# A slot's rows requested two pieces later, plain heads in three groups, logits evicted first, and the values' products in the rows' order

## The chip, the cores and the metric

The kernel runs on one core of a Trainium2 chip. The metric is the device time of one execution in microseconds (us). A core has TensorE (PE; its weight loads are shown apart as PEld), VectorE (DVE), ScalarE (ACT), GpSimd (POOL) and SyncE (SP), which issues most of the transfers.

## The reference

Two parts stand one behind the other. The first is windowed causal attention (8 batches, 8 heads, 576 positions, 64 wide, window 64); the second is a mixture of experts over the resulting 4608 rows of 512, each row going to one of 8 experts.

```python
scores = scale * np.matmul(q, k.transpose(0, 1, 3, 2))
mask = (rel >= 0) & (rel < window)                     # rel = row - column, window 64
attn = softmax(np.where(mask, scores, -1e9))           # with 1e-9 added to the sum
x = matmul(attn, v).transpose(0, 2, 1, 3).reshape(B * S, H * D)
logits = x @ w_gate + modality_bias[modality_id]
e_idx = np.argmax(logits, axis=1)
gate_w = softmax(logits)[np.arange(N), e_idx]
for e in range(E):
    mask = e_idx == e
    h = np.maximum(x[mask] @ w1[e], 0.0)
    out[mask] = gate_w[mask, None] * (h @ w2[e])
```

w1 is 512x1024 and w2 1024x512 for each expert. The expert's products are computed in three parts each (high times high, high times low, low times high), so that the result has nearly fp32 precision.

## The kernel before

**Attention.** The 4608 rows are 72 blocks of 64, nine to a batch; two blocks are a pair (36 pairs), two pairs a group (18 groups, `G`). The main loop (`for s in range(NPR + 4)`) is a pipeline over the pairs: step `s` computes the products with the values for pair `s - 2` (`values`, then `values_out`, which divides by the sums and writes the row tile `xa`), the logits of pair `s - 3` (`logits`), the scores of pair `s` (`scores`, and `minima` on VectorE), the transposes of the probabilities of pair `s - 1` (`probs_t`, two sets of four, each copied out by ScalarE as `pT`), and the exponentials on ScalarE (`exps`), in three portions. It also turns the heads of group `G = s // 2 + 1`: `PARTS` has k's two parts in an even step and q's two in an odd one. The first of the two goes over TensorE (`heads_t`, four transposes) and a copy out of PSUM (`heads_out`).

**Heads.** `load_qk` loads the k or q of one group. Below group 8 (`QUARTERS`), all eight heads come as plain rows, two transfers for each batch that the group touches. From group 8 on only the first four heads do (`nh = HP`); the other four come as quarters in eight transfers of 32-column pieces for each batch touched, laid out so that one VectorE transpose (`turn_heads`) turns the whole second part. Groups 11, 13 and 15 (of those from 8 on) hold a batch's end, touch two batches, and so have twenty transfers for k and as many for q.

**Rows.** The rows of `xa` are kept in an order of 32-column pieces; with it a VectorE transpose of 32x32 blocks (`x_turn`) later gives the transposed row tile of a slot. `values` writes the heads in their natural order, and `values_out` puts them into the rows' order with two products, one for each half of a head. The logits select an expert (`route1` to `route3`), and GpSimd scatters each pair's rows to the expert's place in `xs_scratch` by an indirect transfer.

**Slots.** A slot is 256 rows of one expert. `slot_pieces` is a generator of TensorE work: `first(sl, k, i)` is an eighth of the first product (12 matmuls of 256 columns), `second(sl, k, t)` an eighth of the second (6 of 512 columns). A slot has 16 pieces. From step 12 (`FIRST`) on, every step takes four of them at fixed places (`gap`). A slot's rows are read from `xs_scratch` by `fetch`, which calls `load_slot`: a register load of the row number and five transfers, all on SP, into `xt` (one buffer). Ahead of them `fetch` has the VectorE instructions of the plan issued that give the row number (`tick(need - issued[0], table=True)`). Then `x_turn` turns the tile on VectorE, and `x_part` splits it into a high and a low part (`xh`, `xl`). The first slots (`EARLY`) are taken while attention runs, and the rest (`LATE`) behind it; `last` tells the generator which.

**Order.** The order of the instructions on each engine is written out by hand (`manual_schedule`); each engine runs its own list in order, and so does SP with its transfers. `weights(s)` is one step in loading, splitting and storing a piece of the first two experts' weights: it has the piece before stored (`split_lo`, VectorE), the next one's high part made (`split_hi`, ScalarE, line 114) and another loaded (`load_piece`, SP, lines 103 and 107). The PSUM pool `ps_t` has two banks; `turn_bank` hands them out from step 12 on to the logits, the two sets of probabilities, the rows of `x_t`, the heads' transposes and the ranks.

Lines that come up below: 266 `x_turn`, 287 the gate's copy out of `xt`, 313 `hl`, 467 TensorE's transposes, 561 `turn_heads`, 577 and 583 the plain and the quarter loads, 598 `heads_out`, 633 scores, 668 `pT`, 685 the values' products, 691 and 696 `values_out`, 713 and 718 the logits and their eviction.

Of the kernel before, what the change touches and what calls it, by code (L numbers as in the profile page):

```python
# [8 lines left out]
F32 = mybir.dt.float32  # L9
# [4 lines left out]
ALU = mybir.AluOpType  # L14
# [5 lines left out]
P = 128  # L20
W64 = 64
# [5 lines left out]
def tile_window_attn_moe(  # L27
# [240 lines left out]
    def slot_pieces():  # L268
# [140 lines left out]
        while True:  # L409
            nxt = None  # L410
            for k in range(1, NK):
                for i in range(2):
                    if (k, i) == ((1, 0) if last else (2, 1)) or k == 2 and i == 1 and nxt is None:
                        assert todo
                        nxt = fetch()
                    first(sl, k, i)
                    if k == NK - 1 and i == (0 if last else 1):
                        later.append(lambda: x_turn(nxt))
                    yield
                for t in range(2):  # L420
                    second(sl, k - 1, t)
                    if k == NK - 1 and nxt and t == 1:
                        x_part(nxt, 1)
                    yield
                    if k == NK - 1 and nxt and t == 0:
                        x_part(nxt, 0)
                        run_later()
            second(sl, NK - 1, 0)
            yield
            if nxt["nb"] == 1:  # L430
                break
            first(nxt, 0, 0)
            yield
            first(nxt, 0, 1)
            yield
            second(sl, NK - 1, 1)
            yield
            sl = nxt
# [103 lines left out]
    def new_qk(G, nm):  # L542
# [4 lines left out]
        else:  # L547
            qk[G, nm] = work.tile([P, 2, H, D], F32, name="qk", bufs=2)

    def plain(t, nh):  # L550

        return t.rearrange("p t h d -> p (t h d)")[:, 0:2 * nh * D].rearrange("p (t h d) -> p t h d", t=2, d=D)
# [12 lines left out]
    def load_qk(G, nm, blocks=range(GBLK), dma=nc.sync):  # L565

        t = qk[G, nm]
        x = q if nm == "q" else k
        i = blocks[0]
        while i <= blocks[-1]:  # L570
            b, g = divmod(GBLK * G + i, BPB)
            n = min(BPB - g, blocks[-1] + 1 - i)
            nh = H if G < QUARTERS else HP
            src = x[b, 0:nh, g * W64:(g + n) * W64].rearrange("h (p t) d -> p t h d", t=2)
            p0 = i * W64 // 2
            for par in range(2):
                dma.dma_start(out=plain(t, nh)[p0:p0 + n * W64 // 2, par], in_=src[:, par])
            u = slice(i * W64 // R32, (i + n) * W64 // R32)
            for h in range(nh, H):
                for c in range(2):  # L580
                    rows = slice((h % 2 * 2 + c) * R32, (h % 2 * 2 + c + 1) * R32)
                    src = x[b, h, g * W64:(g + n) * W64, c * R32:(c + 1) * R32]
                    dma.dma_start(out=by_heads(t)[rows, (h - nh) // 2, u, :],
                                  in_=src.rearrange("(u p) d -> p u d", p=R32))
            i += n

    def heads_t(G, nm, i, tp):


        src = plain(qk[G, nm], H if G < QUARTERS else HP).rearrange("p t (h a) d -> p t h (a d)", a=2)  # L590
        for h in range(2):
            for t in range(2):
                n = 2 * h + t
                turn(tp[:, n * P:(n + 1) * P], src[:, t, 2 * i + h])
# [79 lines left out]
        nc.gpsimd.tensor_scalar(out=rs, in0=sm, scalar1=1e-9, scalar2=None, op0=ALU.add)  # L674


    def values(p):
        st.pop((p, "s"))
        av = st[p, "av"] = ps_a.tile([P, H, D], F32, name="av")
        for u in range(H):  # L680
            a, hp = divmod(u, HP)
            pT = st[p, "p", a]
            for c in range(2):
                i = hp * P + c * W64
                nc.tensor.matmul(  # L685
                    out=av[c * W64:(c + 1) * W64, 2 * hp + a], lhsT=pT[:, i:i + W64],
                    rhs=(vo if c else ve)[p][:, 2 * hp + a, :], start=True, stop=True)

    def values_out(p):
        rs = st.pop((p, "rs"))  # L690
        nc.vector.reciprocal(out=rs, in_=rs)
        xa = st[p, "xa"] = xas[p % XBUF]
        av = st.pop((p, "av")).rearrange("p (c g) (a d) -> p a c g d", g=2, a=2)
        to = xa[:, 0:DM].rearrange("p (g a c d) -> p a c g d", g=2, a=2, d=R32)
        for a in range(2):
            nc.vector.tensor_tensor(  # L696
                out=to[:, a], in0=av[:, a],
                in1=rs.rearrange("p (c g) -> p c g", g=2)[:, :, :, None].broadcast_to([P, NC1, 2, R32]), op=ALU.mult)

    def x_t(p, xp):  # L700
        xa = st[p, "xa"]
# [337 lines left out]
    for s in range(NPR + 4):  # L1039
# [10 lines left out]

        if 2 <= s < NPR + 2:
            values(s - 2)
            values_out(s - 2)
        if 3 <= s < NPR + 3:
            logits(s - 3, turn_bank(s) if s != FIRST else ps_m.tile([P, 512], F32, name="y0"))
            if (s - 3) % GB == GB - 1:
                route1((s - 3) // GB)
        if s < NPR:
            scores(s)
            if s == FIRST:  # L1060
# [50 lines left out]
        if n_gap > 2:  # L1111
            if FIRST <= s < FIRST + 4:
                weights(s)
            gap(it, True)
        if heads and G >= QUARTERS:
            turn_heads(G, *heads[1])
        elif heads:
            tp = turn_bank(s)
# [288 lines left out]
```

## Time and profile before

| | |
|---|---|
| median of 3 runs | 633.24 us (632.9 to 634.61) |
| profiled execution | 633.95 us |
| its span, first to last instruction | 632.2 us |
| mean granted TensorE clock | 0.985 |
| TensorE busy | 601.1 us (95%) |
| VectorE, ScalarE, GpSimd busy | 390.4, 294.3, 139.5 us |
| share of 16 DMA engines, SP's queue | 44.6% |
| steps 2 to 11 (attention alone) | 18.2 to 74.4 us |
| steps 12 to 36 (attention and slots) | 74.4 to 347.9 us |
| the rest (slots alone, with the last logits) | 347.9 to 632.2 us |

In a timeline row stand the start, the duration, the engine, the line, the operation, the tiles (out<-in), the shape and the count, and in brackets the engine's idle time before it and what ended it. In a row of waits stand who waited and for what, then the total, the number and the longest. In a row of stretches stand the stretch and its length, then each engine's busy time with its number of instructions, then the granted clock, the share of the DMA engines and GB/s. TensorE's matmuls overlap, so that the distance between two starts, not the duration, is what one costs in a row of many.

### The profile page before, as it was taken

The numbers are of one execution on the slowest core, as the hardware profiler recorded it, in microseconds if no ns is written. First come the engines' busy times: TensorE is split into PE (matmuls) and PEld (weight loads), VectorE is DVE, ScalarE is ACT, GpSimd is POOL, SyncE is SP. The second block draws the span as 40 slices with busy tenths as digits, with TensorE's granted clock in tenths as the row PEclk, the third lists the DMA queues.
The fourth block names the chain that finished last, engine by engine and source line by source line (L and its number), as shares of the span: only waits on it lengthen the run. The fifth ranks groups of instructions, "written<-read, shape, count | busy, mean of one in ns | idle before, by whom it ended". The sixth has DMA issues, their size and how long they took to land.

```text
span 632.2 us, 17434 instructions
## 1 busy us (share of the span) xinstructions
PE 601.1 (95%) x6285; PEld 536.4 (85%) x6285; DVE 390.4 (62%) x1532; ACT 294.3 (47%) x923; POOL 139.5 (22%) x315
## 2 busy tenths in 40 slices
PE   8999879699999989999999999999999999999996
PEld 5888678588889869888888999999899999989985
DVE  3899988587877767867765365223323634876721
ACT  3899786556565645555545111111113422564411
POOL 6332422132032312222321220011011101102202
PEclk7999999989999989999999999999999999999999
DMA  8999855765467457456532232732062554688300
GB/s 163 204 236 244 216 133 153 175 169 126 101 176 180 107 148 167 120 117 143 137 92 59 77 101 70 223 110 51 28 190 68 167 167 117 191 243 245 122 13 25
DMA packets 182793, 88.10 MB, mean 139 GB/s; under 512 B 146426, under 2 KB 165424, under 8 KB 182576
## 3 DMA queue, kind: packets, MB, share of 16 engines
q1 hardware_dynamic: 174080, 67.46, 44.6%
q0 software_dynamic: 5888, 18.93, 8.0%
q8 instruction: 50, 0.82, 0.5%
q10 hardware_dynamic: 2736, 0.58, 0.5%
q14 instruction: 39, 0.32, 0.2%
HBM read 67.49 MB, written 23.91 MB: 145 GB/s over the span
## 4 chain that ended last, share of the span: by engine, by line
PE 50%; DVE 0%; issue 0%; POOL 0%; ACT 0%; POOLq 0%
PE y L326 23%; PE em L304 13%; PE sp L304 10%; PE tp L467 1%; PE y L377 1%; PE av L685 1%; PE sp L352 0%; PE em L352 0%; PE tp L713 0%; PE sp L633 0%; DVE xa L696 0%; POOL out_dram L390 0%; ACT pT L668 0%; POOLq L1284 0%; DVE y L388 0%
## 5 line engine op out<-in xcount | busy, mean ns | idle before, releaser
L326 PE MATMUL y<-Whi,hh 128*128 128x512 f32 x288 | 116.2, 403 | 0.0
L659 ACT ACTIVATE ss<-ss,mn 128x128 f32<-128x128 f32 x288 | 112.5, 396 | 5.2 <-DMA y<-in_moe_modality_id_dram 2.7
L326 PE MATMUL y<-Wlo,hh 128*128 128x512 f32 x288 | 113.6, 395 | 0.0
L326 PE MATMUL y<-Whi,hl 128*128 128x512 f32 x288 | 113.0, 392 | 0.0
L337 POOL DMA_INDIRECT out_dram<-y,id x36 | 39.8, 1104 | 235.2 <-DVE y L334 154.9
L313 DVE SCALAR_TENSOR_TENSOR hl<-em,hh 128x512 fp32r<-128x512 f32 x50 | 34.5, 689 | 87.2 <-ACT hh L312 86.6
L304 PE MATMUL em<-xh,Whi 128*128 128x256 f32 x400 | 83.8, 291 | 0.0
L304 PE MATMUL em<-xl,Whi 128*128 128x256 f32 x400 | 79.2, 279 | 0.0
L304 PE MATMUL em<-xh,Wlo 128*128 128x256 f32 x400 | 79.1, 279 | 0.0
L312 ACT ACTIVATE hh<-em 128x512 fp32r<-128x512 f32 x50 | 29.6, 591 | 105.3 <-PE em L304 101.4
L668 ACT COPY pT<-tp 128x512 f32<-128x512 f32 x57 | 32.3, 588 | 73.6 <-PE tp L467 73.5
L647 DVE CUSTOM_DVE_ANT_0 ss<-sp,masks 128x128 f32<-128x128 f32 x288 | 63.4, 285 | 5.0 <-PE sp L633 4.9
L326 PEld LDWEIGHTS y<-Whi,hl 128*128 128x128 f32 x288 | 54.7, 190 | 12.2
L304 PEld LDWEIGHTS em<-xh,Whi 128*128 128x128 f32 x400 | 62.5, 189 | 1.8
L326 PEld LDWEIGHTS y<-Whi,hh 128*128 128x128 f32 x288 | 54.6, 190 | 9.0
L326 PEld LDWEIGHTS y<-Wlo,hh 128*128 128x128 f32 x288 | 54.8, 190 | 8.5
L304 PEld LDWEIGHTS em<-xl,Whi 128*128 128x128 f32 x400 | 60.9, 188 | 0.1
L304 PEld LDWEIGHTS em<-xh,Wlo 128*128 128x128 f32 x400 | 60.8, 188 | 0.0
L659 ACT ACTIVATION_READ_ACCUMULATOR ss<-ss,mn 128x1 f32 x288 | 55.5, 193 | 0.0
L789 POOL DMA_INDIRECT xs_scratch<-xa,idx x36 | 36.3, 1009 | 74.7 <-DVE lm L732 21.6
L312 ACT ACTIVATE hh<-sp 128x512 fp32r<-128x512 f32 x22 | 13.2, 598 | 75.8 <-PE sp L304 75.8
L467 PE MATMUL tp<-ident_r,ss 128*128 128x128 f32 x236 | 36.1, 284 | 12.3 <-ACT pT L668 8.4
(242 smaller groups left out, 1199.8 us busy)
## 6 DMA issues: line engine op xcount, KB each, us to landing
xt<-xs_scratch SPq DMA_DIRECT2D x72, 128.0 KB, 3.0
vo<-in_v_dram SPq DMA_DIRECT2D x32, 256.0 KB, 3.0
y<-in_moe_w_dram SPq DMA_DIRECT2D x32, 256.0 KB, 3.4
vo<-in_moe_w_dram SPq DMA_DIRECT2D x24, 256.0 KB, 4.1
ss<-in_moe_w_dram SPq DMA_DIRECT2D x24, 256.0 KB, 4.4
xs_scratch<-xs_scratch SPq DMA_DIRECT2D x8, 514.0 KB, 5.9
pT<-in_moe_w_dram SPq DMA_DIRECT2D x16, 256.0 KB, 4.4
qk<-in_k_dram SPq DMA_DIRECT2D x18, 128.0 KB, 4.7
```

What stands on the lines that cost most here:

```text
L304: nc.tensor.matmul(out=hb[:, i * TP:(i + 1) * TP], lhsT=w[buf][:, c0:c0 + P], rhs=x[:, c * TP:(c + 1) * TP], start=(n == 0), stop=(n == le ...
L312: nc.scalar.activation(out=hh, in_=hb, func=AF.Relu),
L313: nc.vector.scalar_tensor_tensor(out=hl, in0=hb, scalar=0.0, in1=hh.bitcast(F32), op0=ALU.max, op1=ALU.subtract)))
L326: nc.tensor.matmul(out=sl["y", t], lhsT=h[:, i * TP + t * P:i * TP + (t + 1) * P], rhs=w[buf][:, c0:c0 + DM], start=(k == 0 and n == 0), s ...
L337: ins = nc.gpsimd.indirect_dma_start(out=out, out_offset=bass.IndirectOffsetOnAxis(ap=sl["id"][:, t:t + 1], axis=0), in_=y, in_offset=None ...
L377: nc.tensor.matmul(out=yp[:, cols], lhsT=sl["h", n][lo][:, c * P:(c + 1) * P], rhs=w[buf][:, c0 + cols.start:c0 + cols.stop], start=(m == ...
L467: nc.tensor.transpose(out=out_, in_=in_, identity=ident[p0:p0 + n, p0:p0 + n])
L647: nc.vector.tensor_tensor_reduce(out=ss[a][:, hp, :], in0=sp[a][:, hp * P:(hp + 1) * P], in1=mask, scale=-1.0 / 8.0, scalar=3.0e38, op0=AL ...
L659: nc.scalar.activation(out=ss[a][:, hp, :], in_=ss[a][:, hp, :], func=AF.Exp, bias=mn[:, h:h + 1], scale=-1.0, accum_out=sm[:, h:h + 1])
L668: nc.scalar.copy(out=pT, in_=pp)
L685: nc.tensor.matmul(out=av[c * W64:(c + 1) * W64, 2 * hp + a], lhsT=pT[:, i:i + W64], rhs=(vo if c else ve)[p][:, 2 * hp + a, :], start=Tru ...
L789: ins = nc.gpsimd.indirect_dma_start(out=xs, out_offset=bass.IndirectOffsetOnAxis(ap=idx[:, j:j + 1], axis=0), in_=xg[j], in_offset=None)
```

## The change

It has four parts.

1. The request of the next slot's rows (`fetch`), while attention runs, stands ahead of `second(sl, 1, 1)` and no longer ahead of `first(sl, 2, 1)`: two pieces later. `x_turn` stays where it was. Behind attention nothing moves.
2. A new function `quartered(G)` tells whether a group's second part comes as quarters: from group 8 on, unless the group holds a batch's end. So groups 11, 13 and 15 load all heads plain, with four transfers each for k and q, and turn their second parts on TensorE, with a copy on ScalarE (k) or VectorE (q).
3. In the steps behind `FIRST`, `values_out` comes behind the logits, their eviction and `route1`; up to `FIRST` it stays ahead of them.
4. `values` writes each head's product in two runs of 32 columns to the places that the rows' order gives them in the bank. `values_out` then needs one product over 512 columns, with the reciprocals written out once for each run of 32 (`rw`, 16 values a row).

```diff
@@ slot_pieces
-                    if (k, i) == ((1, 0) if last else (2, 1)) or k == 2 and i == 1 and nxt is None:
-                        assert todo
+                    if k == 1 and i == 0 and last:
                         nxt = fetch()
+                        turn_at = 0
                     first(sl, k, i)
-                    if k == NK - 1 and i == (0 if last else 1):
+                    if k == NK - 1 and i == turn_at:
                         later.append(lambda: x_turn(nxt))
                     yield
                 for t in range(2):
+                    if k == 2 and t == 1 and nxt is None:
+                        nxt = fetch()
+                        turn_at = 1
                     second(sl, k - 1, t)
...
+    def quartered(G):
+        return G >= QUARTERS and GBLK * G // BPB == (GBLK * G + GBLK - 1) // BPB
@@ load_qk
-            nh = H if G < QUARTERS else HP
+            nh = HP if quartered(G) else H
@@ heads_t
-        src = plain(qk[G, nm], H if G < QUARTERS else HP).rearrange("p t (h a) d -> p t h (a d)", a=2)
+        src = plain(qk[G, nm], HP if quartered(G) else H).rearrange("p t (h a) d -> p t h (a d)", a=2)
...
+    def by_block(x):
+        return x.rearrange("p h d -> p (h d)").rearrange("p (g a c d) -> p g a c d", g=2, a=2, d=R32)
@@ values
-                    out=av[c * W64:(c + 1) * W64, 2 * hp + a], lhsT=pT[:, i:i + W64],
-                    rhs=(vo if c else ve)[p][:, 2 * hp + a, :], start=True, stop=True)
+                    out=by_block(av)[c * W64:(c + 1) * W64, a, :, hp, :], lhsT=pT[:, i:i + W64],
+                    rhs=(vo if c else ve)[p][:, 2 * hp + a, :].rearrange("p (a d) -> p a d", a=2),
+                    start=True, stop=True)
@@ values_out
-        nc.vector.reciprocal(out=rs, in_=rs)
+        rw = small.tile([P, 2, 2, HP], F32, name="rw")
+        nc.vector.reciprocal(
+            out=rw, in_=rs.rearrange("p (c g) -> p g c", g=2)[:, :, None, :].broadcast_to([P, 2, 2, HP]))
         xa = st[p, "xa"] = xas[p % XBUF]
-        av = st.pop((p, "av")).rearrange("p (c g) (a d) -> p a c g d", g=2, a=2)
-        to = xa[:, 0:DM].rearrange("p (g a c d) -> p a c g d", g=2, a=2, d=R32)
-        for a in range(2):
-            nc.vector.tensor_tensor(
-                out=to[:, a], in0=av[:, a],
-                in1=rs.rearrange("p (c g) -> p c g", g=2)[:, :, :, None].broadcast_to([P, NC1, 2, R32]), op=ALU.mult)
+        nc.vector.tensor_tensor(
+            out=xa[:, 0:DM].rearrange("p (x d) -> p x d", d=R32),
+            in0=st.pop((p, "av")).rearrange("p h d -> p (h d)").rearrange("p (x d) -> p x d", d=R32),
+            in1=rw.rearrange("p g a c -> p (g a c)")[:, :, None].broadcast_to([P, 2 * H, R32]), op=ALU.mult)
@@ the main loop
             values(s - 2)
-            values_out(s - 2)
+            if s <= FIRST:
+                values_out(s - 2)
         if 3 <= s < NPR + 3:
             logits(s - 3, turn_bank(s) if s != FIRST else ps_m.tile([P, 512], F32, name="y0"))
             if (s - 3) % GB == GB - 1:
                 route1((s - 3) // GB)
+        if FIRST < s < NPR + 2:
+            values_out(s - 2)
...
-        if heads and G >= QUARTERS:
+        if heads and quartered(G):
             turn_heads(G, *heads[1])
```

## The prediction

> **What bounds the kernel now.** I read the page's first part, then the stretches of single steps, then TensorE's waits, and then, wait by wait, the timelines of the engines that ended them.
>
> ```profile
> span 632.2 us, 17434 instructions
> PE 601.1 (95%) x6285; PEld 536.4 (85%) x6285; DVE 390.4 (62%) x1532; ACT 294.3 (47%) x923; POOL 139.5 (22%) x315
> ...
> 74.39:85.23 10.84, 8.32 (x125) 7.51 (x124) 10.55 (x47) 8.75 (x35) 3.92 (x8) 1.00 0.65 175
> ...
> 97.47:107.47 10.00, 10.00 (x133) 9.03 (x132) 7.86 (x43) 5.63 (x21) 2.85 (x4) 1.00 0.70 176
> 117.94:136.29 18.35, 12.60 (x133) 10.71 (x132) 11.55 (x46) 8.50 (x31) 4.88 (x9) 0.81 0.61 146
> ...
> 220.61:235.78 15.17, 12.20 (x138) 10.33 (x137) 8.57 (x38) 6.46 (x22) 2.86 (x5) 0.89 0.51 140
> 277.93:287.93 10.00, 10.00 (x133) 9.03 (x132) 5.75 (x29) 5.00 (x20) 3.45 (x7) 1.00 0.68 153
> ```
>
> The stretches run from one pair's first product with the values to the next pair's: steps 12, 14, 16, 25 and 30. A step of the shared stage (attention beside the first slots) takes 10.00 us where TensorE never idles (steps 14 and 30). Step 16 takes 18.35 and step 25 takes 15.17, at a granted clock of 0.81 and 0.89. So the stage is TensorE's own work plus a list of stalls, and the change can pay only out of that list, or by TensorE's work.
>
> ```profile
> PE tp L467 <- ACT pT L668: 10.4, 7, 5.0
> PE tp L467 <- DVE lg L718: 3.8, 7, 1.4
> PE tp L467 <- DMA qk<-in_q_dram: 2.3, 2, 2.0
> PE sp L633 <- DVE se L775: 0.8, 1, 0.8
> ```
>
> These four rows of TensorE's waits between 74 and 348 us (total, times, longest) hold 17.3 of its idle time; the clock that drops after the two long ones adds to them. Behind 348 us TensorE is almost without gaps, and no edit changes that part's order, except that its first row loads come from the moved request.
>
> **Logits first (C).** In every step behind 12 the eviction of `lg` now stands ahead of `values_out` on VectorE.
>
> ```profile
> 238.07 0.88 DVE L696 TENSOR_TENSOR xa<-av,rs 128x256 f32<-128x256 f32 x2
> 238.87 0.15 DVE L718 TENSOR_TENSOR lg<-tp,bias_sel 128x8 f32<-128x8 f32 x1
> ...
> 239.17 0.52 PE L467 MATMUL tp<-ident_r,ss 128*128 128x128 f32 x3 [0.20 <-DVE lg L718]
> ...
> 181.72 0.59 ACT L668 COPY pT<-tp 128x512 f32<-128x512 f32 x1 [2.68 <-PE tp L467]
> 182.36 0.66 PE L467 MATMUL tp<-ident_r,ss 128*128 128x128 f32 x4 [0.68 <-ACT pT L668]
> 182.66 0.15 DVE L718 TENSOR_TENSOR lg<-tp,bias_sel 128x8 f32<-128x8 f32 x1
> ```
>
> In step 26 `lg` ends at 239.02, and the second set of probability transposes starts at 239.17: it takes the bank that the logits held. With the eviction ahead of the reciprocal and the two products it ends some 1.1 us earlier (238.07 to 238.87, and about 0.3 for the reciprocal), more than nearly all of the seven waits; I take 3.5 of their 3.8. In step 21 the second set starts at 182.36, 0.05 after the copy of the first set has ended (181.72 + 0.59) and ahead of `lg`: there it shares the first set's bank. The row of 10.4 is five such waits of 0.68, one of 5.0 (step 16) and one of 2.0 (step 12). Whether the earlier eviction makes the second set take the logits' bank there the trace can't say: between 0 and 3.4; one of the five goes with B, of the other 2.7 I take half, 1.4. VectorE must now wait for the logits (0.5 us behind the values' products) in steps where it is early; its row products then end later, but their reader `x_t` comes one scores' set and a piece later on TensorE, and the minima wait for the scores anyway. If VectorE were late in all steps, `x_t` would be next to wait. C: 4.9, bounds 3 to 7.
>
> **Plain heads (B).** With `QUARTERS` = 8, the groups 11, 13 and 15 hold a batch end. Each part's load (k or q) is now 4 issues on SP and not 20.
>
> ```profile
> 222.98 4.89 SPq L583 DMA_DIRECT2D qk<-in_q_dram  x8
> 227.91 1.26 SPq L577 DMA_DIRECT2D qk<-in_q_dram  x2
> ...
> 230.39 0.30 PE L467 MATMUL tp<-ident_r,qk 128*128 128x128 f32 x1 [2.01 <-DMA qk<-in_q_dram]
> 230.98 0.87 PE L467 MATMUL tp<-ident_r,qk 128*128 128x128 f32 x3 [0.29 <-DMA qk<-in_q_dram]
> ...
> 236.05 0.71 DVE L561 STREAM_TRANSPOSE qT<-qk 128x512 f32<-128x512 f32 x1 [2.67 <-DMA qk<-in_q_dram]
> ```
>
> Eight quarter issues take 4.89 us, so 16 fewer save SP 9.8 us a part. In group 13 the plain issues of the second batch (227.91) stand behind the quarters of the first, and TensorE stalls 2.01 + 0.29 for them in step 25. Ahead of them they go out some 4.9 us earlier, more than the stall. The clock of 0.89 over 15.17 us is worth (1 - 0.89) x 15.17 = 1.7 at most; of it I take 1.2. Step 25's wait of 0.68 for a late VectorE goes too, since VectorE no longer waits for quarters there. Gain 2.3 + 1.2 + 0.7 = 4.2.
>
> What it adds: four transposes on TensorE for each second part, six sets in all.
>
> ```profile
> 242.90 0.60 PE L467 MATMUL tp<-ident_r,qk 128*128 128x128 f32 x4
> 243.25 0.47 PE L326 MATMUL y<-Whi,hh 128*128 128x512 f32 x1
> ```
>
> A set holds TensorE from 242.90 to 243.25, 0.35, and the matmul behind it takes 0.08 more (0.47 against the usual 0.39): 0.43 x 6 = 2.6, all of it on TensorE's path, since these steps have no other idle time. The copies (about 0.6 each, one on ScalarE and one on VectorE) replace a VectorE transpose of the same size; both engines have room in the step (VectorE 5.75 of 10.00 in the last stretch above). If it is gone, the next logits wait for the bank. B: 4.2 - 2.6 = 1.6, bounds -2.6 to 2.5.
>
> **The later request (A).** Five row loads per slot and the register load ahead of them move past one weight piece on SP, sometimes two, but not past the next step's loads of v, k and q; the forced ticks on VectorE move with them.
>
> ```profile
> 109.53 3.87 SPq L211 DMA_DIRECT2D xt<-xs_scratch  x5
> 113.67 0.36 SPq L107 DMA_DIRECT2D y<-in_moe_w_dram  x1
> 114.28 0.34 SPq L103 DMA_DIRECT2D y<-in_moe_w_dram  x1
> ...
> 117.00 3.95 SPq L583 DMA_DIRECT2D qk<-in_k_dram  x8
> 121.21 2.46 SPq L103 DMA_DIRECT2D y<-in_moe_w_dram  x3
> ...
> 124.92 0.62 ACT L114 CAST Whi<-y 128x512 fp32r<-128x512 f32 x1 [5.66 <-DMA y<-in_moe_w_dram]
> ...
> SPq L211 <- DMA xs_scratch<-xa,idx: 8.4, 3, 4.5
> ```
>
> SP stands 4.5 us for the rows' scatter before it issues the rows at 109.53; the weights wait behind. ScalarE then stands 5.66 us at 124.92 for the piece issued at 121.21, and that is TensorE's 5.0 in step 16. Now the pieces of 113.67 and 114.28 go out while SP would have stood. But the rows can't go before 109.5 (the scatter is no earlier), and the piece of 121.21 still follows the rows, v and ten issues of k. It moves up by what left the queue ahead of it: 109.53 + 3.87 = 113.40 to 114.75, about 1.3. So of the 5.0 only 1.2 goes; the 0.8 at the scores (VectorE behind a late piece) goes too. A: 2.0, bounds -3 to 6.
>
> What it puts at risk is the rows' arrival ahead of `x_turn`:
>
> ```profile
> 207.87 0.19 POOL L287 COPY gate<-xt 128x2 f32<-128x2 f32 x1 [7.87 <-DMA xt<-xs_scratch]
> ...
> 208.50 1.29 DVE L266 STREAM_TRANSPOSE xt<-xt 128x512 f32<-128x512 f32 x2
> ```
>
> GpSimd's copy shows the landing, 0.63 ahead of the transpose, the tightest that I found. Here SP lags the program by more than a step, so it issues the rows only one weight piece later (0.6); and B takes away the lag that groups 11 and 13 put on SP. I cost it at nothing.
>
> **The rows' order (D).** VectorE's two products of 128x256 become one of 128x512, the reciprocal writes 16 values, not 8.
>
> ```profile
> L696 DVE TENSOR_TENSOR xa<-av,rs 128x256 f32<-128x256 f32 x72 | 30.6, 425 | 10.1 <-PE av L685 4.9 <-DMA xs_scratch<-xa,idx 1.0 <-PE sp L633 0.4
> ...
> L313 DVE SCALAR_TENSOR_TENSOR hl<-em,hh 128x512 fp32r<-128x512 f32 x50 | 34.5, 689 | 87.2 <-ACT hh L312 86.6
> ...
> 246.17:247.67 1.50, 1.15 (x32) 1.01 (x32) 1.00 0.67 151
> ...
> 44.65:74.39 29.74, 27.98 (x156) 1.00 0.95 234
> ```
>
> Two by 425 are 0.85 (0.88 in the pair at 238.07); the nearest row of the new size out of PSUM takes 0.69. So 0.19 less a step. It counts where VectorE bounds: step 12 has it busy 10.55 of 10.84, and steps 7 to 11 (last row, VectorE alone) 27.98 of 29.74. Some seven steps there give 7 x 0.19 = 1.3; further on it is cover. Bounds 0 to 2.3 (twelve steps).
>
> On TensorE the values' products (third row, line 685 alone: 32 matmuls, 1.15 us, beside 1.01 of weight loads) now write two runs of 32 columns, 128 apart. No row of this trace has a matmul with a broken output. Between nothing and each counting as two: 0 to 36 x 1.15 = 41 us. I take nothing, since the weight loads already fill 1.01 of the 1.15 and the runs are 32 long.
> [...]
>
> **The sum.** C 4.9 + B 1.6 + A 2.0 + D 1.3 = 9.8. The profiled execution took 633.95 (span 632.2 and 1.75 around it): 633.95 - 9.8 = 624.2. It stands 0.7 above the median of the runs, 633.24, from which the same gain gives 623.4; I say 624.
>
> **Rivals.** *The stalls move on.* TensorE gains at the logits and waits again: VectorE is still late, the second set stays in the first set's bank, the extra copies of B hold a bank. For it: step 16's reason stays in the queue, and a step can't go under 10.00. Against it: 10.00 is reached in steps whose VectorE has 7.86 of work. It leaves D, half of C and A's 0.8, less B's 2.6: about 2 off, 631 to 632.
>
> *The broken output costs TensorE time* (slower than before). One mechanism, line 685: 576 pairs of matmuls; it decides from 9.8 / 576 = 17 ns a pair, where a pair now takes 1.15 / 16 = 72 ns. Doubled it costs 41: 633.2 - 9.8 + 41 = 664; at half of that 644. [...]
>
> *The rows come late.* If they land five us later than now (two pieces of a step of 10 with four) at all six slots of the stage, the margin of 0.6, perhaps of 3 at others, is gone, VectorE stands about 2 us a slot ahead of `hl` and the minima, and TensorE behind it: 6 x 2 = 12, so 633.2 - 9.8 + 12 = 635. Against it: SP's lag decides the issue, not the program.
>
> **Chances.** Forecast 0.70; stalls move on 0.16; broken output 0.07; late rows 0.07. The measurement tells about 0.3%, 1.9 us. Faster: 0.70 and half of the second, 0.78; same 0.10; slower 0.12. The range: below, the upper bounds of C, B and A with D (7 + 2.5 + 6 + 1.3 = 16.8) give 616.4, and not all come together: 617; above it takes in the moved stalls, 633, and leaves out the two slower ones.
>
> **What would show it.** C: `lg` ahead of `rw` in each step, and TensorE's row for `lg` near zero; the 0.68 waits gone or still there. B: no quarter issues in groups 11, 13, 15, step 25 under 11 us at clock 1.00, TensorE's transposes of `qk` up by 24. A: step 16 at 15 to 17 us, ScalarE's wait for `y` down by 1 to 2 in all; `x_turn` with no wait for a DMA. D: line 685 still 1.15 us a step, one product of 0.69. Wrong it would be if line 685 takes over 1.4 us, if `xt` shows DMA waits, or if step 16 loses its stall whole.

## The result, and the profile after

| | before | after |
|---|---|---|
| median of four runs each, one chip | 633.07 us (632.88 to 634.61) | 622.82 us (621.75 to 625.21) |
| ratio to before, 95% interval | | 0.9838 (0.9802 to 0.9874) |
| profiled execution, span | 633.95, 632.2 us | 621.75, 620.0 us |
| mean granted TensorE clock | 0.985 | 0.995 |
| steps 12 to 36 | 273.5 us | 262.7 us |

The forecast was 624.0. In the changed kernel the lines have moved a little: 470 TensorE's transposes, 640 scores, 675 `pT`, 696 the values' products, 704 and 707 the reciprocal and the product of `values_out`, 730 the eviction of the logits, 787 the sums that the scores wait for.

First the head of the page of the changed kernel, then the stretches of its steps 12, 14, 16, 21, 24 and 25 (stretch and length, busy time by engine, granted clock, share of the DMA engines, GB/s):

```profile
span 620.0 us, 17351 instructions
...
PE 596.6 (96%) x6309; PEld 534.8 (86%) x6309; DVE 385.8 (62%) x1493; ACT 293.6 (47%) x926; POOL 138.6 (22%) x315
```

```profile
73.03:83.56 10.53, 8.11 (x125) 7.44 (x125) 10.21 (x44) 8.43 (x34) 4.09 (x8) 1.00 0.72 192
...
94.94:104.94 10.00, 10.00 (x133) 9.04 (x132) 7.10 (x36) 5.99 (x21) 2.86 (x4) 1.00 0.81 200
115.08:131.26 16.18, 11.54 (x134) 10.07 (x133) 10.03 (x43) 7.06 (x25) 4.30 (x8) 0.89 0.60 145
172.34:183.92 11.58, 10.85 (x142) 9.58 (x141) 8.57 (x36) 6.91 (x24) 3.50 (x8) 1.00 0.71 188
204.09:215.44 11.35, 10.67 (x137) 9.41 (x136) 8.54 (x42) 7.13 (x25) 3.51 (x6) 1.00 0.73 193
215.44:226.08 10.64, 10.64 (x141) 9.60 (x140) 9.31 (x44) 6.32 (x23) 2.88 (x6) 1.00 0.51 126
```

TensorE has 24 more transposes and yet is busy 4.5 us less. Of that 2.0 lies in steps 12 to 36 (253.62 for 255.57), where a clock of 0.81 in step 16 and 0.89 in step 25 had stretched it before (12.60 and 12.20 us busy, now 11.54 and 10.64); 1.8 lies ahead of step 2 (13.40 for 15.22, at a clock of 1.00 for 0.81). The changed kernel's second profile has 15.85 at 0.74 there, so that part is not the change's. Step 25 has gone from 15.17 us at a clock of 0.89 to 10.64 at 1.00, all of it TensorE's own work; step 16 from 18.35 at 0.81 to 16.18 at 0.89; a free step is 10.00 as before. Steps 21 and 24 have become longer, by 0.5 and 0.4. What TensorE still waits for between 74 and 340 us (total, times, longest):

```profile
PE tp L470 <- ACT pT L675: 8.1, 4, 4.6
PE tp L470 <- DVE lg L730: 0.5, 1, 0.5
PE y L725 <- DVE se L787: 0.4, 1, 0.4
```

The row for the logits' eviction is down from 3.8 to 0.5, the two for `qk` and for the scores are gone. Timeline rows of the changed kernel, in order of time: VectorE in step 15, the queue and its readers in step 16, the second set of probabilities in steps 21 and 24, and the rows of step 23:

```profile
107.37 0.14 DVE L730 TENSOR_TENSOR lg<-tp,bias_sel 128x8 f32<-128x8 f32 x1
107.45 0.23 DVE L704 RECIPROCAL rw<-rs 128x16 f32<-128x16 f32 x1
107.71 0.69 DVE L707 TENSOR_TENSOR xa<-av,rw 128x512 f32<-128x512 f32 x1
...
113.13 3.95 SPq L590 DMA_DIRECT2D qk<-in_k_dram  x8
117.32 2.08 SPq L103 DMA_DIRECT2D y<-in_moe_w_dram  x3
...
120.71 0.62 ACT L114 CAST Whi<-y 128x512 fp32r<-128x512 f32 x1 [5.79 <-DMA y<-in_moe_w_dram]
...
122.91 1.11 PE L470 MATMUL tp<-ident_r,ss 128*128 128x128 f32 x4 [4.64 <-ACT pT L675]
...
174.47 0.16 DVE L730 TENSOR_TENSOR lg<-tp,bias_sel 128x8 f32<-128x8 f32 x1
...
175.62 0.59 ACT L675 COPY pT<-tp 128x512 f32<-128x512 f32 x1 [2.74 <-PE sp L640]
...
176.26 0.66 PE L470 MATMUL tp<-ident_r,ss 128*128 128x128 f32 x4 [0.73 <-ACT pT L675]
...
196.97 2.44 SPq L211 DMA_DIRECT2D xt<-xs_scratch  x5
...
201.83 0.19 POOL L287 COPY gate<-xt 128x2 f32<-128x2 f32 x1 [7.11 <-DMA xt<-xs_scratch]
...
202.88 1.29 DVE L266 STREAM_TRANSPOSE xt<-xt 128x512 f32<-128x512 f32 x2
...
207.96 0.66 PE L470 MATMUL tp<-ident_r,ss 128*128 128x128 f32 x4 [0.68 <-ACT pT L675]
```

`lg` stands ahead of the reciprocal, and one product of 0.69 has taken the place of two. In step 16 the weight piece (117.32) still follows the ten k issues of group 9, ScalarE still stands 5.79 us for it and TensorE 4.64. In step 21 `lg` is out at 174.63, and the second set waits all the same until the first set's copy is done (175.62 + 0.59 = 176.21): it takes the first set's bank, not the logits'. In step 23 GpSimd's copy shows the rows there 1.05 before `x_turn` (201.83 for 202.88), which has no wait. The first slot turned behind step 12, in step 15, has less to spare: 0.37, where the kernel before had 3.28.

Where the 12.2 us of span went, step by step: start -0.5; steps 2 to 11 -0.8; 12 -0.3; 13 -0.9; 15 -0.3; 16 -2.2; 17 -0.5; 20 -0.6; 21 +0.5; 24 +0.4; 25 -4.5; 26 -0.4; 28 and 29 -0.5; 32 and 33 -0.9; 36 -0.7. The part behind step 36 is the same to 0.1 us (284.4 and 284.3). In the 14 profiles of this case the time before step 2 varies from 16.4 to 19.5 us, so its 0.5 says nothing of the change, and steps 2 and 7 together from 10.0 to 11.7, so not much of the 0.8 can be read here either.

### The profile page after: what moved, and what is told of

Same layout as the page of the kernel before. It is cut to its first block, busy times and chain, and to the rows that moved or that the text cites. A ratio compares the mean times of both kernels' runs of the same rounds, so it can differ in the third digit from the quotient of the medians.

```text
span 620.0 us, 17351 instructions
## 1 busy us (share of the span) xinstructions
PE 596.6 (96%) x6309; PEld 534.8 (86%) x6309; DVE 385.8 (62%) x1493; ACT 293.6 (47%) x926; POOL 138.6 (22%) x315
## 4 chain that ended last, share of the span: by engine, by line
PE 82%; ACT 3%; issue 1%; DVE 1%; DMA 1%; POOL 0%; POOLq 0%; ACTq 0%; DVEq 0%
PE y L326 32%; PE em L304 22%; PE sp L304 10%; PE tp L470 8%; PE av L696 4%; PE sp L640 3%; PE tp L725 2%; PE y L377 1%; ACT ss L666 1%; DMA y<-in_moe_w_dram 1%; PE sp L352 0%; PE em L352 0%; ACT pT L675 0%; DVE xt L266 0%; ACT Whi L114 0%
## 5 line engine op out<-in xcount | busy, mean ns | idle before, releaser
L696 PEld LDWEIGHTS av<-ve,pT 128*64 128x64 f32 x576 | 36.3, 138 | 12.9 <-issue 7.4
```

The lines of the kernel that those rows point to most:

```text
L696: nc.tensor.matmul(out=by_block(av)[c * W64:(c + 1) * W64, a, :, hp, :], lhsT=pT[:, i:i + W64], rhs=(vo if c else ve)[p][:, 2 * hp + a, :] ...
```

## The experiments

The diffs are against the changed kernel, that of `e12_late_alone` against the kernel before. Ratios are to the kernel before, measured beside each experiment on the same chip; its median was 634.96 beside `e1` to `e4`, 636.29 beside `e5` to `e8`, and 634.47 beside `e9` to `e12`.

**The changed kernel once more** (`e5_again`), beside `e6` to `e8`.

> The changed kernel once more, unaltered, so that steps 12, 16 and 21 of a second profile and the time on this chip can be set beside the others. Both theories: 621 to 625 us; if step 16 differs from 16.2 by over 1 us, the 2 us that the earlier runs put on the later request can't be read off one profile.

624.18 us (621.45 to 627.06), ratio 0.9812 (0.9781 to 0.9842). From step 12 on all steps but a few repeat to 0.02 us; 16 (16.26 for 16.18), 21 (12.18 for 11.58), 12 and the time before it (start of step 12 at 74.36 for 73.03) do not. `e2_no_plain` and `e7_plain13` (below) differ from the changed kernel only from group 11's loads on, behind step 18; yet their step 12 takes 14.60 and 10.40, and their step 16 takes 17.27 and 17.23. So nothing below 4.2 us is read from step 12 in that list, and nothing below 1.1 from step 16, whose length also goes with its clock (16.18 at 0.89, and 18.13 at 0.81 in `e8_stride8`; last section).

**Logits first, undone** (`e3_no_first`).

```diff
             values(s - 2)
-            if s <= FIRST:
-                values_out(s - 2)
+            values_out(s - 2)
...
-        if FIRST < s < NPR + 2:
-            values_out(s - 2)
```

> The changed kernel with values_out ahead of the logits again in all steps; the other three parts stay. My theory: the waits of TensorE for lg and for the first set's copy come back in steps 13, 15, 17, 20, 26, 28, 29, 32, 33 and 36: 5 to 6 us more. Rival: the one product (0.2 less a step) and VectorE's freedom from quarters removed most of these waits; then 1 to 2 us more.

629.47 us (628.67 to 630.39), ratio 0.9914 (0.9893 to 0.9936), against 0.9838 and 0.9812 with the part in. TensorE's waits in this kernel, and the second set that waits for the first copy in step 20 (step 36 has the same wait):

```profile
PE tp L470 <- ACT pT L675: 9.0, 6, 4.4
PE tp L470 <- DVE lg L730: 2.6, 4, 1.3
```

```profile
169.89 0.66 PE L470 MATMUL tp<-ident_r,ss 128*128 128x128 f32 x4 [0.68 <-ACT pT L675]
```

Waits for the logits go from one to four, and waits for `pT` from four to six. The steps 13, 15, 16, 17, 19, 20, 23, 25, 28, 29, 32, 33 and 36 are longer, 6.7 in all, and 5.8 without step 16, which varies by as much. So the earlier eviction is one of the two parts that carry the gain (plain heads is the other) and is shown by its own removal. Some of it shows in no wait of the list: steps 17, 19, 23, 29, 32 and 33 are 0.3 longer each. In all six `lg` ends 3.1 to 3.2 us into the step (2.1 to 2.3 in the changed kernel), and the second set starts right behind it, at 3.3 for 3.0. TensorE's matmuls overlap (in the trace before, a set of four lasts 0.60, and the matmul behind it starts 0.35 after the set does), so the trace counts only 0.1 of this as idle.

**The rows' order, undone** (`e4_no_order`): `values` writes heads of 64 columns one behind the other, and `values_out` has two products of 256.

```diff
-                    out=by_block(av)[c * W64:(c + 1) * W64, a, :, hp, :], lhsT=pT[:, i:i + W64],
-                    rhs=(vo if c else ve)[p][:, 2 * hp + a, :].rearrange("p (a d) -> p a d", a=2),
+                    out=av[c * W64:(c + 1) * W64, 2 * hp + a], lhsT=pT[:, i:i + W64],
+                    rhs=(vo if c else ve)[p][:, 2 * hp + a, :],
...
```

> The changed kernel with the values' products in the heads' natural order and two products on VectorE; the other three parts stay. My theory: 1.1 to 1.5 us more, all of it by step 14 (steps 6 to 13, where VectorE bounds); the values' 32 matmuls take 1.15 us in both. Rival 1: later steps lose too, since VectorE comes 0.2 later to the logits: 3 us more. Rival 2: the broken output costs TensorE time; then the 32 matmuls take less here and the run is not slower.

626.33 us (624.4 to 627.06), ratio 0.9857 (0.9832 to 0.9882). Steps 2 to 11 take 56.36 us (18.06 to 74.42), against 55.37 and 54.89 with the part in (the changed kernel and `e5_again`); behind step 12 only 16 and 21 differ, which vary anyway. But the 1.0 to 1.5 can't be read off these sums: `e1_no_late`, with the part in, takes 56.44, and `e8_stride8`, with two products, 55.13. The steps that repeat say more: 6 and 8 to 11 together take 30.46 to 30.49 in all four kernels with two products (the one before, this one, `e8_stride8`, `e12_late_alone`) and 29.3 to 30.3, 29.87 in the mean, in the ten with one. So the part is worth 0.6 in the mean there, where attention runs alone; the ratios can't tell it from nothing.

**Columns eight apart** (`e8_stride8`): an output in runs of one column and not of 32, so that no two neighbouring columns of a product are neighbours in the bank. `values_out` has two products again.

```diff
-                    out=by_block(av)[c * W64:(c + 1) * W64, a, :, hp, :], lhsT=pT[:, i:i + W64],
+                    out=av.rearrange("p h d -> p (h d)").rearrange("p (e h) -> p e h", h=H)[
+                        c * W64:(c + 1) * W64, :, 2 * hp + a], lhsT=pT[:, i:i + W64],
...
```

> The changed kernel, but each of the values' products writes its 64 columns 8 apart (no two neighbours), and VectorE divides with two products, gathering from there. If runs of neighbours matter to TensorE's writes, the 32 matmuls of a step take well over 1.15 us, up to 2.3, and the run 20 to 40 us more; if not, 1.15 us as before, and some 2 to 4 us more for the second product on VectorE.

625.44 us (623.8 to 626.42), ratio 0.9825 (0.9794 to 0.9856). The line of the values' products (times in ns: least, median, most), first in this kernel, then in the changed one, then in the one before:

```profile
L696 PE MATMUL av<-ve,pT x576: 222/222/271, 19.1 to 339.9; 128*64 128x64 f32 x192
```

```profile
L696 PE MATMUL av<-ve,pT x576: 222/222/271, 17.7 to 336.7; 128*64 128x64 f32 x192
```

```profile
L685 PE MATMUL av<-ve,pT x576: 222/222/270, 18.2 to 348.8; 128*64 128x64 f32 x192
```

Contiguous, in two runs of 32, or in single columns eight apart: the same, and a step's 32 products take 1.15 us in each. A rival of the prediction falls here for this size. The 2 to 4 us expected for the second product did not come either: the changed kernel, measured beside it (`e5_again`), has 624.18.

**The later request, undone** (`e1_no_late`).

```diff
-                    if k == 1 and i == 0 and last:
+                    if (k, i) == ((1, 0) if last else (2, 1)) or k == 2 and i == 1 and nxt is None:
                         nxt = fetch()
-                        turn_at = 0
+                        turn_at = 0 if last else 1
...
-                    if k == 2 and t == 1 and nxt is None:
-                        nxt = fetch()
-                        turn_at = 1
```

> The changed kernel with the request of the slot's rows back at its old place; the other three parts stay. My theory: the later request is worth what step 16 gained: step 16 goes from 16.2 us back to about 18.3, the other steps stay, the profiled time is about 624 (changed kernel 621.75), 2 us more. Rival: step 16's gain came from VectorE being earlier (logits first, one product) and from SP's shorter queue; then step 16 stays within 0.5 of 16.2 and the time within 1 us of the changed kernel.

624.01 us (621.82 to 625.57), ratio 0.9828 (0.9802 to 0.9854): not to be told from the changed kernel. By the ratios the time came out as the rival said. The profiled run (624.24) and step 16 (18.61) came out as the theory said, but the changed kernel's second profile has 623.69 too, and step 21 is 0.9 shorter here (10.65).

**The later request alone** (`e12_late_alone`), in the kernel before: the diff above the other way round, and nothing else.

> The kernel before with the later request alone; quarters, order of the logits and the two products as before. Theory of the prediction: 2 us less than before, in step 16. Rival, from the run without plain heads: SP, late by the quarters of group 11, issues the rows after one more weight piece, VectorE waits 3 to 5 us at x_turn and TensorE in step 24 behind it: step 24 at 15 to 17 us (10.9 before), and 1 to 5 us more than before in all.

635.61 us (632.86 to 637.12), ratio 1.0014 (0.9995 to 1.0033): no gain. Its steps 16, 24, 25 and 26, and `x_turn` of the slot whose rows are used in step 24:

```profile
117.71:134.60 16.89, 12.01 (x133) 10.37 (x132) 10.47 (x44) 7.17 (x25) 4.76 (x9) 0.80 0.59 144
208.71:223.11 14.40, 12.06 (x133) 10.17 (x132) 10.64 (x45) 6.80 (x23) 4.68 (x10) 0.88 0.46 108
223.11:236.21 13.10, 10.79 (x138) 9.24 (x137) 7.97 (x37) 6.49 (x23) 1.92 (x5) 1.00 0.47 126
236.21:247.93 11.72, 10.42 (x134) 9.01 (x133) 7.56 (x38) 5.23 (x20) 4.02 (x7) 1.00 0.71 157
```

```profile
210.44 1.30 DVE L266 STREAM_TRANSPOSE xt<-xt 128x512 f32<-128x512 f32 x2 [2.86 <-DMA xt<-xs_scratch]
```

It takes 1.5 less in step 16 (which varies by that much) and 2.1 less in step 25, and 3.5 more in step 24 and 1.3 more in step 26. The rows come late, as one rival said: VectorE stands 2.86 us for them.

**Plain heads, undone** (`e2_no_plain`): groups 11, 13 and 15 have quarters again.

```diff
-        return G >= QUARTERS and GBLK * G // BPB == (GBLK * G + GBLK - 1) // BPB
+        return G >= QUARTERS
```

> The changed kernel with quarters again in groups 11, 13 and 15; the other three parts stay. My theory: step 25 goes from 10.6 back to about 15 us with TensorE's wait for q of some 2.3 and the clock's drop, the six sets of transposes (2.6 us in steps 20, 21, 24, 25, 28, 29) go: about 2.4 us more in all. Rival: the rows' later request already freed SP ahead of group 13; then step 25 stays under 12 us, and the run is 2 to 2.6 us less than the changed kernel.

630.92 us (628.05 to 636.85), ratio 0.9943 (0.9915 to 0.9971). The loss of 7 to 8 us by the ratios is more than the part was priced at, and it does not lie where I expected it: step 25 is 11.07 and not 15, but step 24 is 16.96; steps 24 to 29 together are 7.5 longer than in the changed kernel. (Step 12 is 14.60; it is one of those that vary, and lies ahead of these groups' loads.) Stretches of steps 24 and 25, VectorE's wait for the rows, and TensorE's waits behind it:

```profile
207.24:224.20 16.96, 12.88 (x133) 10.79 (x132) 10.57 (x44) 7.26 (x25) 4.63 (x10) 0.80 0.56 131
224.20:235.27 11.07, 10.39 (x137) 9.19 (x137) 8.03 (x36) 6.39 (x23) 1.97 (x5) 1.00 0.49 128
```

```profile
210.72 1.30 DVE L266 STREAM_TRANSPOSE xt<-xt 128x512 f32<-128x512 f32 x2 [4.61 <-DMA xt<-xs_scratch]
```

```profile
PE tp L470 <- ACT pT L675: 10.1, 4, 4.8
PE sp L640 <- DVE se L787: 3.9, 2, 3.4
```

The rows are the ones that lie ready 1.05 ahead in the changed kernel. Here VectorE stands 4.61 us for them, TensorE 3.4 at the scores behind VectorE, and the clock falls to 0.80.

**Plain heads in group 13 alone** (`e7_plain13`): is it group 13's second batch, as I had argued, or group 11's quarters, which stand ahead of those rows?

```diff
-        return G >= QUARTERS and GBLK * G // BPB == (GBLK * G + GBLK - 1) // BPB
+        return G >= QUARTERS and G != 13
```

> The changed kernel with plain heads in group 13 alone (quarters in 11 and 15). Theory 1, from the prediction: groups 11 and 15 had no stall, so four sets of transposes less: 1.7 us less than the changed kernel. Theory 2, from the run without plain heads: group 11's quarters make SP late, the rows requested later land behind x_turn's place in step 23, VectorE waits 3 to 5 us and TensorE behind it in step 24: 2 to 5 us more than the changed kernel.

626.55 us (626.03 to 627.72), ratio 0.9845 (0.982 to 0.987). Step 25 is 10.64, but it was 11.07 with no plain heads at all, where TensorE comes late out of step 24 and finds q landed; so this run does not show group 13's own share. Step 24 is 16.37. Two of group 11's four runs of quarters, then the queue ahead of the rows and `x_turn`; below them group 11's load of k in the changed kernel:

```profile
159.53 4.23 SPq L590 DMA_DIRECT2D qk<-in_k_dram  x8
...
173.52 5.31 SPq L590 DMA_DIRECT2D qk<-in_q_dram  x8
...
196.19 6.29 SPq L590 DMA_DIRECT2D qk<-in_q_dram  x8
...
204.06 2.99 SPq L211 DMA_DIRECT2D xt<-xs_scratch  x5
...
209.21 1.30 DVE L266 STREAM_TRANSPOSE xt<-xt 128x512 f32<-128x512 f32 x2 [4.60 <-DMA xt<-xs_scratch]
```

```profile
157.57 2.08 SPq L584 DMA_DIRECT2D qk<-in_k_dram  x4
```

The eight issues of 6.29 us at 196.19 are not group 11's: they are q of group 12, which has quarters in the changed kernel too (3.96 us at 185.60). Group 11's k holds the queue from 158.48 to 169.97 here, 11.5 us where four plain issues take 2.1, and its q another 12.3 for 3.8. So group 12's quarters start 10.6 later, and the rows go out at 204.06 and not at 196.97; the changed kernel's queue stands idle from 190.19 until then. Group 11's plain heads, and the slack that they leave on the queue, are what keeps the rows in time.

**The same with the old request** (`e9_plain13_early`): the diffs of `e7_plain13` and `e1_no_late` together.

> Plain heads in group 13 alone, and the request of the rows back at its old place; logits first and the rows' order stay. Theory 1 (the later request makes the rows late once group 11's quarters hold SP): VectorE's wait of 4.6 us at x_turn and TensorE's of 3.4 in step 24 go, step 24 is 11.4 us or less, the profile 5 us under that of plain heads in group 13 with the later request (627.52): 621 to 623. Theory 2 (group 11's quarters make it late by themselves): step 24 stays near 16 and the time at 626 to 627.

625.29 us (622.95 to 629.31), ratio 0.9861 (0.9826 to 0.9896). Step 24 takes 14.45, and `x_turn` waits:

```profile
209.63 1.30 DVE L266 STREAM_TRANSPOSE xt<-xt 128x512 f32<-128x512 f32 x2 [2.61 <-DMA xt<-xs_scratch]
```

That lies between the two theories. In the changed kernel group 11's quarters make the rows late with either request (2.61 us); the later request adds 2.0 (4.60).

**Plain heads in group 9 as well** (`e6_plain9`). Step 16's weight piece follows the quarters of group 9, which holds no batch's end; plain, it has two issues a part and not ten, and costs TensorE eight transposes more.

```diff
-        return G >= QUARTERS and GBLK * G // BPB == (GBLK * G + GBLK - 1) // BPB
+        return G >= QUARTERS and G != 9 and GBLK * G // BPB == (GBLK * G + GBLK - 1) // BPB
```

> The changed kernel with group 9 plain too (it loads in steps 15 and 16). My theory: what is left of step 16's stall (4.6 us and the clock behind it) is the weight piece behind group 9's eight quarter issues of k, 3.9 us of SP; with them gone the stall falls under 1 us, step 16 to 11 or 12 us, two sets of transposes cost 0.86: 3.5 to 4.5 us less than the changed kernel. Rival: the piece waits for its buffer or for the DMA engines, the stall stays; then 0.5 to 1 us more.

621.32 us (619.5 to 623.37), ratio 0.9769 (0.9746 to 0.9792). Its step 16, the queue and ScalarE there, and TensorE's wait:

```profile
115.72:128.46 12.74, 10.70 (x138) 9.43 (x137) 9.57 (x42) 7.68 (x26) 3.77 (x8) 1.00 0.62 164
```

```profile
112.50 1.92 SPq L584 DMA_DIRECT2D qk<-in_k_dram  x2
114.67 2.64 SPq L103 DMA_DIRECT2D y<-in_moe_w_dram  x3
...
118.76 0.62 ACT L114 CAST Whi<-y 128x512 fp32r<-128x512 f32 x1 [3.19 <-DMA y<-in_moe_w_dram]
...
120.95 0.66 PE L470 MATMUL tp<-ident_r,ss 128*128 128x128 f32 x4 [2.04 <-ACT pT L675]
```

The wait falls from 4.64 to 2.04, the clock stays at 1.00, and step 16 is 3.4 us shorter than in the changed kernel (step 17 is 0.55 longer by the added transposes). So the queue's order is shown to be most of what was left in step 16; I had expected a wait under 1 us and a step of 11 to 12. ScalarE still stands 3.19 for the piece.

**The remaining two combinations**: plain heads in 9 and 13 only with the old request (`e10_plain9_13_early`), and plain heads in 9, 11, 13 and 15 with the old request (`e11_plain9_early`).

> Plain heads in groups 9 and 13 alone, the request at its old place; logits first and the rows' order stay. If the later request only matters through the row loads' place on SP, this takes the 3.5 us of plain heads in group 9 in step 16 and saves four sets of transposes (1.7 us) that groups 11 and 15 don't need: 618 to 620 us, the fastest of all. If the old request costs its 2 us in step 16 here too: 620 to 622.

> Plain heads in groups 9, 11, 13 and 15, the request at its old place; logits first and the rows' order stay. Beside the same with the later request (621.32 median, step 16 at 12.7 us) it prices the later request alone where no group holds SP: theory of the prediction, 2 us more, in step 16; rival, within 1 us and step 16 within 0.7 of 12.7, so that the later request is worth nothing that can be told.

`e10_plain9_13_early`: 622.04 us (618.98 to 623.93), ratio 0.9807 (0.9777 to 0.9837); just past the upper of the two expectations. Step 24 is 12.86, with `x_turn` standing 2.45 us for its rows, so that the spared transposes of groups 11 and 15 are paid for there: that wait is again behind group 11's quarters. `e11_plain9_early`: 620.49 us (617.14 to 621.2), ratio 0.9773 (0.9744 to 0.9801), the same as `e6_plain9`. Against `e6_plain9`, with the later request, step 16 is 1.9 longer (14.65, at a clock of 0.88) and step 12 is 2.9 longer (13.27 for 10.40, where `x_turn` stands 1.2 us for its rows), but step 12 starts 2.1 earlier and step 21 is 0.9 shorter (10.65 for 11.58). So the time is as the rival said and step 16 as the theory said; but its wait is 2.12 us, that of `e6_plain9` 2.04, and the difference lies in the clock, 0.88 in the one step and 1.00 in the other (last section). These two, with four groups plain, are the fastest kernels measured, 0.4 to 0.7% under the changed one by the ratios; their intervals and that of `e5_again` still overlap.

## Why the prediction was right

The time, 622.82, is 1.2 under the forecast, and the profiled execution came down by 12.2 where the sum said 9.8, with 0.5 of it ahead of step 2. The mechanisms of the early eviction and of the shorter queue are borne out; that the sum came so near is in part luck, since one of its terms is worth nothing that can be measured, one half of what it said, and one far more.

**Logits first.** Forecast 4.9. Of the 3.8 for `lg`, 3.3 went. Of the five waits of 0.68, three went (steps 25, 29 and 36); without this part step 36 has its wait again and step 20 one too, while 25 and 29 stay without: so two fall to it, as I had taken (1.4), one of them in another step. Its removal costs more than these, 5.8 by the steps without step 16 and 4.8 to 6.5 by the ratios, since it also brings the 0.3 in six steps that the list of waits leaves out: the term was about right, or too small by up to 1.6. What I could not say the built programs answer, for each use of the two banks has its bank fixed there, before anything runs. The second set has the first set's bank in steps 16, 21, 24, 25, 29 and 36 of the kernel before, in 16, 21 and 24 of the changed one, and in 16, 20, 21, 24 and 36 with this part undone. TensorE's waits for `pT` behind step 12 lie in just these steps; the long one of step 16 is among them, because the first set's copy stands behind ScalarE's wait for the weight piece. So the second set can stay in the first set's bank although `lg` is out long before (1.6 us in step 21). That much of the rival in which the stalls move on came true. Why the build chooses the banks so stays open.

**Plain heads.** Forecast 4.2 - 2.6 = 1.6. Step 25 came down by 4.5 with one added set in it, more than worked out, and the price of 0.43 a set was right: steps 20, 28 and 29 take 10.34, 10.02 and 10.18 in `e7_plain13`, where they have no such set, and 10.78, 10.46 and 10.66 in `e5_again`, where they have one. With the other five sets at 0.43 that is 2.4 net. But the step of the argument that says where the gain lies was incomplete. I counted group 13's second batch; group 11 has no stall of its own in the trace before, and I gave it only a cost. `e2_no_plain` and `e7_plain13` show that its quarters hold the queue some 18 us longer (11.5 and 12.3 for 2.1 and 3.8), and that in the new kernel the rows of step 23 would be 4.6 us late behind them. By the ratios the part is worth 7 to 8 us inside the change, not 1.6 and far outside the bounds that I gave it, -2.6 to 2.5.

**The later request.** Forecast 2.0, as 1.2 of step 16's wait and 0.8 at the scores. Step 16 came down by 2.2 and the 0.8 is gone, but the wait fell only from 4.99 to 4.64, and ScalarE's own wait did not fall (5.66 and 5.79): the piece goes out 3.9 earlier (117.32 for 121.21) mostly because the whole step starts 2.9 earlier. So of the 2.2 the wait is 0.35, the scores 0.8, and the rest TensorE's own work, 11.54 for 12.60, at a clock of 0.89 for 0.81. In eight profiles with the later request and group 9 in quarters step 16 took 16.2 to 19.4, in three with the old one 18.4 to 19.3; step 21 took 11.6 to 12.8 with it, 10.65 to 11.8 without: in `e1_no_late` and `e11_plain9_early`, at 10.65, the built program gives the second set of step 21 the logits' bank, in the changed kernel the first set's. So the term of 2.0 was right in size for this profile only by chance: by the ratios (0.9838 and 0.9812 with, 0.9828 without; 0.9769 with, 0.9773 without) the part is worth nothing that can be measured, and alone it is worth nothing either (1.0014). Its risk was named rightly, "B takes away the lag that groups 11 and 13 put on SP": where B is not there (`e12_late_alone`, `e2_no_plain`) the rows are 2.9 and 4.6 late. The rival had priced that at 2 us in six slots; it is one slot of the stage that pays, with 3.5 to 5.6 us in one step.

**The rows' order.** Forecast 1.3; 0.6 in the mean in the five steps of attention alone that repeat, so the term was about twice too big. I had named the reciprocal's 16 values for 8 and left them out of the sum. The reciprocal's groups, before and after:

```profile
L691 DVE RECIPROCAL rs<-rs 128x8 f32<-128x8 f32 x36 | 7.0, 194 | 0.4
```

```profile
L704 DVE RECIPROCAL rw<-rs 128x16 f32<-128x16 f32 x36 | 8.8, 244 | 0.4
```

So by the means 0.11 a step is saved (0.85 + 0.194 - 0.691 - 0.244) and not 0.19, which over five to seven steps is 0.5 to 0.8. The values' products cost nothing more, as I had taken it: 222 ns in the median of line 696 in the changed kernel, and 222 with the columns eight apart (`e8_stride8`), as in the kernel before. My 41 us for each product counting as two, and the 664 and 644 of the rival, were an estimate from the 1.15 us of a step; no run shows any of it.

## What to carry to other kernels

Where one queue issues everything in order, as SP's does here, a transfer's place behind many small issues can decide when it lands (the rows of step 23 went out at 204.06 us in `e7_plain13` and at 196.97 in the changed kernel), and shortening the queue can matter most for a transfer that waits for nothing yet (these rows are there 1.05 us ahead in the changed kernel; in `e2_no_plain` VectorE stands 4.61 us for them): ask for every part of a change what it protects, not only which wait it removes. A step's wait was worth more than its own length where the clock fell behind it (step 25 came down by 4.5 us without its waits of 2.01, 0.29 and 0.68, at a clock of 1.00 for 0.89), and behind like waits it fell in one profile and not in another (0.88 with 2.12 us in `e11_plain9_early`, 1.00 with 2.04 in `e6_plain9`), so one profile does not price such a wait. Where a pool has two banks, read from the built program which use gets which. Undo each part of a bundle by itself, and do it alone as well: here one part was priced at 2 us by the rows of before and is worth 7 inside the change, and another nothing that can be measured in either place.

## What was not expected of the hardware

TensorE wrote its 64 columns in single elements eight apart as fast as in one run (222 ns, 1.15 us for 32 products beside 1.01 of weight loads); larger outputs were not tried. The clock did not follow the length of a wait alone: it stayed at 1.00 in a step with a wait of 2.04 us (`e6_plain9`), was 0.89 with one of 4.64, and 0.80 with one of 4.42 in `e3_no_first`; before the change it was 0.89 with 2.01 and 0.29 one behind the other.

The clock's own records, and stretches cut at their bounds, show more. Two stretches of step 16 in the changed kernel, then two in `e6_plain9`:

```profile
118.92:122.33 3.41, 0.00 (x0) 0.00 (x0) 0.45 (x1) 1.62 (x4) 0.00 (x0) 1.00 0.89 235
122.33:125.74 3.41, 2.83 (x9) 2.45 (x10) 3.38 (x21) 1.88 (x7) 0.00 (x0) 0.50 0.75 155
```

```profile
117.11:120.52 3.41, 1.81 (x44) 1.38 (x40) 2.07 (x9) 1.76 (x4) 0.00 (x1) 1.00 0.87 249
120.52:123.93 3.41, 2.98 (x20) 2.67 (x21) 3.36 (x22) 2.25 (x7) 0.00 (x0) 1.00 0.79 181
```

In all 14 profiles the granted clock is 1.00 or 0.50 and, between 65 and 350 us, changes only on a grid of 3.41 us that lies elsewhere in each profile. Step 16's 0.89 in the changed kernel is one interval at half (1 - 0.5 x 3.41 / 16.18), 0.80 in `e3_no_first` two (1 - 0.5 x 6.83 / 17.13). Counted over the 14 profiles, an interval at full clock in which TensorE was busy for 45% or less was followed by one at half in all 17 cases; at 52% or more in none; in between, in three of seven. In the kernel before and the changed one the intervals followed by one at half were busy for 20%, 41% and 0%, and one of 48% was not. The clock came back behind an interval at half in which TensorE was busy for 83% or more, and stayed at 77% or less. So like waits met one such interval or none: that of 2.12 in `e11_plain9_early` one (1 - 0.5 x 3.41 / 14.65 = 0.88), that of 2.04 none, split over two intervals that were busy for 53% and 87%; and of the longer ones that of 4.64 emptied one interval and met one at half, that of 4.42 met two. That it is the place on the grid that decides is my reading of these counts. The ends of matmuls are modelled in these traces, so the bounds are rough.
